# Turning the normalised rows on DVE, ACT and Pool instead of TensorE

## The chip, the cores and the metric

One core of one Trainium2 chip runs the whole program. The metric is the device time of one execution in microseconds, lower is better. All data are 32-bit floats.

## The reference

Attention with softmax over the feature axis of q and over the token axis of k, then a Fourier mix over tokens and channels, a normalisation without weights, and a two-layer channel network:

```python
batch, n_heads, seq, head_dim = (8, 8, 576, 64)        # so d_model = 512
q_s = softmax(q, axis=-1);  k_s = softmax(k, axis=2)   # each with 1e-09 added to the sum
kv = np.einsum('bhsd,bhde->bhse', ...)                 # k_s^T v, 64 x 64 per head
attn = np.einsum('bhsd,bhde->bhse', q_s, kv)
x = attn.transpose(0, 2, 1, 3).reshape(8, 576, 512)
mixed = np.real(np.fft.fft(np.fft.fft(x, axis=1), axis=2))
u = x + mixed
un = (u - u.mean(-1)) / np.sqrt(u.var(-1) + 1e-06)
out = u + np.maximum(un @ w_ch1, 0.0) @ w_ch2          # 512 -> 2048 -> 512
```

## The kernel before

**Groups.** The 8 x 576 rows are cut into nine groups of 512. Groups 0 to 7 (`g`) are 512 rows of one batch each, and group 8 collects the 64 rows that each of the eight batches leaves over. They run in the order 0 to 6, 8, 7; "order" counts the places, from 0. A group lies in SBUF as four tiles of 128 rows x 512 columns, tile `i` = (c, u) with c = i % 2 and u = i // 2, pairs of them in the `x` buffers (`xs` for group 8).

**Two stages per group.** `up` multiplies the normalised rows by the first weight matrix and applies relu; `down` multiplies by the second and adds to u. Both use Strassen's scheme with seven products, run in the order 1, 6, 5, 7, 2, 4, 3. Group 0 is plain. For the others `up` has eight jobs of seven products with right-hand blocks from `unT`, the normalised rows transposed: [128, 7, 2, 256], slots 0 to 3 the four quarters, slots 4, 1, 5 and 6 their differences (`combine`, `combine_last`). From order 2 on, `down` (`deep_down`) uses a second level of Strassen: product 1 alone, and then the units (2,4), (7,6) and (5,3), each of seven products for two members. Its left-hand sums ("A sums", `a_step`, L1407) are made by DVE (and one kind by Pool), and those of the unit (2,4) are written into the old `unT`, which `up` has left by then. So a new `unT`, of which there is one buffer, can be written only when PE has finished that unit.

**Banks.** Products of a unit gather in three PSUM banks: `ba` for 1 and 2, `bb` for 6, 7 and 4, `bc` for 5 and 3. What takes them out: after 1 ACT copies `ba` to `s1` (L1475); after 6 DVE forms u2 = bb + s1, after 7 u3 = bb + s1 and out(3) = bc + u3 (all L1468); after 2 ACT copies `ba` out, out(0) (L1482); after 4 and 3 DVE forms out(2) and out(1). Since product 7 adds into `bb` after 6, and 4 after 7, PE may start 7 only when u2 has been read, and 4 only when u3 has.

**Between the stages.** While PE runs `up` and `down` of one group, the other engines prepare the next one: attention (`keys`, `own_exp`, `own_times_kv`) during `up`, the folds and the Fourier mix (`folded`, `block`, `mix_own`, `mix_shared`) around the start of `down`, and `norm` late in `down`. `norm` takes the mean and variance of the four tiles on DVE (L1165, L1166), one root on ACT for all four (L1169, with a table load), 1/std and -mean/std on DVE (L1172, L1173), the normalised tile on ACT into a buffer `eo` (L1189), four 128x128 transposes of it on PE into PSUM (L1195), one copy on ACT into `unT` (L1204), and then the differences (L1210, L1215).

**Order.** The whole program is one list of (time, step), sorted by time, and each engine executes its own steps strictly in that order:

```python
    steps += [(before + scale * t, step) for t, step in later]
    ...
        for _, step in sorted(steps, key=lambda s: s[0]):
            step()
```

The times are only a script: they set the order of the steps on each engine, and semaphores do the rest. In `deep_down` one unit of script time (a "slot") stands for half a product, so `down` has slots 0 to 8 for product 1, 8 to 22 for (2,4), 22 to 36 for (7,6) and 36 to 50 for (5,3), and the next group's `up` begins at slot 50. Before the change `block` runs from slot 2, the mixes from 12.5, `norm` from 29. For order 1 `down` is a single level of Strassen with eight slots per product, 56 in all; for order 7, the last normalisation, `norm` starts at slot 14 before and after.

**A pattern already there.** `own_exp` turns q in 32x32 tiles on DVE (L764), and carries them to their quadrants of 32 partitions with 16 ACT instructions of 32x128 that also take the exponent (L774). The keys are turned on DVE too (L708).

**Keys and values.** `keys` multiplies the turned keys by values in `vt` (L715): r = 0 and 1 with the first half of the columns, r = 2 and 3 with the second half, which `values_to` loads into the same tile by four DMAs after r = 1.

Of the kernel before, what the change touches and what calls it, by code (L numbers as in the profile page):

```python
# [40 lines left out]
F32 = mybir.dt.float32  # L41
# [5 lines left out]
P = 128  # L47
B, H, S, DH = 8, 8, 576, 64
D = H * DH
# [3 lines left out]
HD = D // 2  # L53
# [5 lines left out]
Q = 32  # L59
W = 2 * Q  # L60
NT = Q // 2 + 1
KT = D // P
VD = 4 * NC - S // Q
NF = FF // P
GT = 4 * P
# [16 lines left out]
UP, TWICE = NP * len(ORDER), 8 + 6 * len(ORDER)  # L82
# [36 lines left out]
def at(t, script):  # L119
    return [(t + dt, step) for dt, step in script]  # L120
# [17 lines left out]
class _Block:  # L138
    def __init__(self, ctx, tc, q, kT, v, w1, w2, ft, cd, out):
# [24 lines left out]

        self.ZT = c.tile([P, KT, P], F32, name="ZT")

# [57 lines left out]
    def turned(self):  # L224
        t = self.ps.tile([P, 4, P], F32, tag="tr", name="tr", bufs=2)
        return t
# [102 lines left out]
    def weights(self):  # L329
# [6 lines left out]
        def fetch(i):  # L336
# [10 lines left out]
            if i < NF:  # L347
                nc.sync.dma_start(raw.rearrange("p (k n) -> p k n", k=KT), w1[:, :, f * 2 * P:(f + 1) * 2 * P])
            else:
# [129 lines left out]
    def attention_timed(self, b, start, end):  # L479

        tail = [("t", b)] if b % 2 == 0 else []
        own = [("q", b, c, u) for c, u in ((0, 0), (0, 1), (1, 1), (1, 0))]
        places, shared = [6, 13.5, 21.5, 27.2], start + 12
        if tail:
            places = [8.5, 14, 21.5, 27.2]
        if start == 0:
            places, shared = [13.5, 20.5, 24, 27.2], 7
        steps = at(start, self.keys(b))
        for it in tail:
            steps += at(shared, self.q_exp(it)) + at(shared + 8, self.t_turn(it))  # L490
            steps += at(22.4 if start < 0 else 35, self.t_fold(it))
        for t, it in zip(places, own):
            steps += at(t, self.own_exp(it)) + at(t + 15, self.own_times_kv(it))
        loads = [(t - 7, t + 7.6, self.own_load(it)) for t, it in zip(places, own)]
        loads += [(shared - 13, shared + 8.4, self.t_load(it)) for it in tail]
        loads.sort(key=lambda s: s[0])
        free = [-99] * 3
        for i, (t, end, load) in enumerate(loads):
            if i > 1:
                steps += at(max(t, free[-3]), load)  # L500
            free.append(end)
        return steps + at((33 if start < 0 else 39) if tail else max(22, start + 26), self.t_times_kv(b))

    def ahead(self, b):


        steps = at(24 if b > 2 else 20, self.keys_to(b))
        steps += at(35 if b > 2 else 22.5, self.values_to(b, 0))
        q = [self.own_load(("q", b, 0, u)) for u in range(2)]
        if b % 2 == 0:  # L510
            q = [self.t_load(("t", b)), q[0]]
        return steps + at(46.5, q[0]) + at(50, q[1])
# [129 lines left out]
    def values_to(self, b, h):  # L642

        def load(i):
            first = VD * (i == 3)
            a = min(i * NC, S // Q - NC) + first
# [5 lines left out]
    def prepare(self):  # L652
# [6 lines left out]
        for col in (0, 2 * P + 1):  # L659
            G.memset(self.vt[:, :, col:col + 1], 1.0)  # L660
        G.memset(self.vt[3 * Q:, 0:VD, :], 0.0)

# [20 lines left out]

        return [(0, copies), (0.3 + 0.15 * (4 // by), least)]

    def keys(self, b):


        nc, V, kb = self.nc, self.nc.vector, self.kb
        box = {}  # L690

        def top(r):
            if r == 0:
                box["m"] = self.small.tile([P, 4 * NR], F32, tag="km16", name="km16", bufs=2)
            V.reduce_max(box["m"][:, 4 * r:4 * r + 4], kb[:, r], axis=AX.X, negate=True)

        def exp(g):
            k = kb[:, g // 4, g % 4]
            nc.scalar.activation(k, k, ACT.Exp, bias=box["m"][:, g:g + 1])

        def turn(r):
            if r == 0:
                t = self.work.tile([P, KT, HD], F32, tag="Z", name="Z", bufs=1)
                t = t[:].rearrange("p k n -> p (k n)")[:, 0:NC * P]
            else:
                t = kb[:, r - 1].rearrange("p g s -> p (g s)")
            to = box["k", r] = t.rearrange("p (c n) -> p c n", n=P)
            V.transpose(to.rearrange("p c (g s) -> p c g s", s=Q), kb[:, r].rearrange("p g (c s) -> p c g s", s=Q))  # L708

        def times(r):  # L710
            pk, k = self.acc((P, P + 1)), box.pop(("k", r))
            box[r] = pk
            a = (P + 1) * (r % 2)
            for c in range(NC):
                nc.tensor.matmul(pk, lhsT=k[:, c, :], rhs=self.vt[:, c, a:a + P + 1], start=c == 0, stop=c == NC - 1)  # L715

        def scale(r):
            pk = box.pop(r)
            rec = self.small.tile([P, 1], F32, tag="krec", name="krec", bufs=4)
            at = P * (r % 2)  # L720
            V.tensor_scalar(out=rec[:], in0=pk[:, at:at + 1], scalar1=ATT_EPS, scalar2=None, op0=ALU.add)
            V.reciprocal(rec[:], rec[:])
            for h in range(2):
                s, cols = slice(64 * h, 64 * h + 64), slice(64 * h + 1 - r % 2, 64 * h + 65 - r % 2)
                V.tensor_scalar(out=self.kvr[b % 2][s, r, s], in0=pk[s, cols], scalar1=rec[s, 0:1], scalar2=None, op0=ALU.mult)

        steps = [(0.9 * r, lambda r=r: top(r)) for r in range(NR)]
        steps += at(3.6, self.across(lambda: box["m"], 2, 4 * NR)) + at(4.5, self.across(lambda: box["m"], 1, 4 * NR))
        steps += [(6 + g / 2, lambda g=g: exp(g)) for g in range(4 * NR)]
        for r in range(NR):  # L730
            for dt, f in ((8.3, turn), (10.8, times), (12.5, scale)):
                steps.append((dt + 2 * r + 6 * (r > 1 and f != turn), lambda f=f, r=r: f(r)))
        steps += at(13.5, self.values_to(b, 1))
        return steps

    def own_load(self, it):
# [330 lines left out]
    def block(self, b, k):  # L1067
# [6 lines left out]
        n = own.stop - own.start  # L1074
        if k == KT:

            own, tail = slice(own.start, own.start + P), slice(tail.start, tail.start + P)

        def times():
            eo, g = self.eo[b], self.live["g", b]  # L1080
            if b not in self.Z:
                self.Z[b] = self.work.tile([P, KT, HD], F32, tag="Z", name="Z", bufs=1)
            full = self.acc((own.stop - own.start, 512))
# [72 lines left out]
    def norm(self, g):  # L1156

        nc, V = self.nc, self.nc.vector
        mv = self.small.tile([P, 4, 2], F32, tag="mv", name="mv", bufs=2)
        std = self.small.tile([P, 4], F32, tag="std", name="std", bufs=2)  # L1160
        uns, box = {}, {}
# [36 lines left out]
        def laid(i):  # L1198
# [4 lines left out]
            copy = V.tensor_copy if g == 0 and c == u else nc.scalar.copy  # L1203
            copy(self.unT[g][:, u:u + 3:2, :, cols], box.pop(i)[:].rearrange("p (a k) t -> p a k t", a=2))  # L1204

        def combine():
            if g > 0:
                some = lambda i: self.unT[g][:, i]
                for e, to, x, y in ((V, 4, 1, 0), (nc.gpsimd, 1, 3, 1), (V, 5, 3, 4)):
                    e.tensor_tensor(out=some(to), in0=some(x), in1=some(y), op=ALU.subtract)  # L1210
# [5 lines left out]

        steps = []
        put = lambda t, f, *a: steps.append((t, lambda: f(*a)))
        if g == 0:
            for some in ((0, 2), (1, 3)):  # L1220
                s = slice(some[0], 4, 2)
                for i in some:
                    put(0, stats, i)
                for f in (root, scales):
                    put(0, f, s)
        else:
            for n, i in enumerate((0, 2, 1, 3)):
                put((0.7, 2.7, 4.7, 6)[n], stats, i)
            s = slice(0, 4)
            put(7.2, root, s)  # L1230
            put(9, scales, s)
            put(13.6, back)
# [391 lines left out]
def kernel(ctx: ExitStack, tc: tile.TileContext, q, kT, v, w1, w2, ft,  # L1624
                                                           cd, out):
    blk = _Block(ctx, tc, q, kT, v, w1, w2, ft, cd, out)

    def timed(t, order, g):
        b = order + 1
        steps = at(t, blk.up(order, g)) + at(t + UP, blk.down(g, order))  # L1630
        if order == B:
            return steps + [(t + 6 + 1.2 * i, lambda i=i: blk.later and blk.later.pop(0)()) for i in range(36)]
        if b == B:
            return steps + at(t + UP + 14, blk.norm(groups[b]))
        start, end = -7 if order > 2 else 0, 45
        if b + 1 < B:
            steps += at(t, blk.ahead(b + 1))
        steps += at(t, blk.attention_timed(b, start, end)) + at(t + end, blk.folded(b))
        t += UP
        for i, k in enumerate((2, 3, 0, 1, 4)):  # L1640
            steps += at(t + 2 + 2 * i, blk.block(b, k))
        mixes = [blk.mix_own(b, c) for c in range(2)]
        if b % 2:
            mixes.insert(0 if b == B - 1 else 2, blk.mix_shared(b // 2))
        for i, some in enumerate(mixes):
            steps += at(t + 12.5 + 3.2 * i, some)
        return steps + at(t + 29, blk.norm(groups[b]))

    fetch, convert = blk.weights()

# [26 lines left out]
    groups = [*range(B - 1), B, B - 1]  # L1677
    first, second, both = 46.9, 56, 77
    steps = blk.opening(fetch, converted)
# [3 lines left out]
    t = first + second  # L1683
# [26 lines left out]
    scale, before = 0.87, t + both  # L1710
    later = []
    t = 0
# [62 lines left out]
```

## Time and profile before

| | us |
|---|---|
| median of 3 runs (range) | 1054.22 (1052.79 to 1058.33) |
| the profiled execution | 1057.53 |
| its span, first to last instruction | 1055.8 |
| PE busy | 1037.7 (98%) |
| PE weight loads busy | 899.8 (85%) |
| DVE busy | 722.6 (68%) |
| ACT busy | 456.1 (43%) |
| Pool busy | 406.0 (38%) |

Matmuls are pipelined, so their durations overlap, and the time that one takes from PE's queue is the step from its start to the next start. A group of both stages takes about 112 us (`down` of order 3 starts at 473.35, that of order 4 at 584.21). Idle time in a row stands with what ended it. "PEld" is PE's weight load; a small q behind an engine is its sequencer.

### The profile page before, as it was taken

The numbers are of one execution on the slowest core, as the hardware profiler recorded it, in microseconds if no ns is written. First come the engines' busy times: TensorE is split into PE (matmuls) and PEld (weight loads), VectorE is DVE, ScalarE is ACT, GpSimd is POOL, SyncE is SP. The second block draws the span as 40 slices with busy tenths as digits, with TensorE's granted clock in tenths as the row PEclk, the third lists the DMA queues.
The fourth block names the chain that finished last, engine by engine and source line by source line (L and its number), as shares of the span: only waits on it lengthen the run. The fifth ranks groups of instructions, "written<-read, shape, count | busy, mean of one in ns | idle before, by whom it ended". The sixth has DMA issues, their size and how long they took to land.

```text
span 1055.8 us, 16768 instructions
## 1 busy us (share of the span) xinstructions
PE 1037.7 (98%) x6178; PEld 899.8 (85%) x6178; DVE 722.6 (68%) x1410; ACT 456.1 (43%) x1141; POOL 406.0 (38%) x350
## 2 busy tenths in 40 slices
PE   8999999899999999999999999999999999999998
PEld 7844555788888899889998999989998998999898
DVE  6898888665566876767765777688657644674563
ACT  5674433672248316751476236821682132131210
POOL 3164320257415645465545643474446450000000
PEclk9999999999999999999999999999999999999999
DMA  9787598586998666855677467757644664576464
GB/s 269 240 281 258 164 257 273 167 251 197 300 308 242 206 217 243 230 190 210 251 236 220 179 239 238 206 201 260 212 170 162 229 243 165 206 259 221 173 222 147
DMA packets 114313, 236.01 MB, mean 224 GB/s; under 512 B 23272, under 2 KB 78696, under 8 KB 103608
## 3 DMA queue, kind: packets, MB, share of 16 engines
q1 hardware_dynamic: 113864, 234.42, 67.7%
q8 instruction: 49, 0.80, 0.3%
q14 instruction: 32, 0.26, 0.1%
q10 hardware_dynamic: 288, 0.26, 0.1%
q0 software_dynamic: 80, 0.26, 0.1%
HBM read 199.79 MB, written 39.06 MB: 226 GB/s over the span
## 4 chain that ended last, share of the span: by engine, by line
PE 78%; DVE 5%; ACT 4%; DMA 3%; issue 1%; SPq 0%; POOL 0%; DVEq 0%; ACTq 0%
PE bb L1334 14%; PE bb L1461 10%; PE ba L1334 10%; PE bc L1334 9%; PE bc L1461 7%; PE ba L1461 7%; PE bb L1431 5%; PE acc L715 3%; ACT qT L774 2%; PE bb L1550 2%; PE acc L790 2%; PE acc L1087 1%; PE acc L1090 1%; DMA vt<-in_v_dram 1%; PE bc L1550 1%; PE ba L1550 1%
## 5 line engine op out<-in xcount | busy, mean ns | idle before, releaser
L1334 PE MATMUL bb<-unT,big 128*128 128x256 f32 x768 | 183.1, 381 | 0.1
L1334 PEld LDWEIGHTS bb<-unT,big 128*128 128x128 f32 x768 | 144.7, 191 | 19.9 <-DVE u L1304 1.0
L1346 ACT ACTIVATE big<-big 128x512 f32<-128x512 f32 x96 | 60.3, 629 | 170.8 <-DVE big L1345 169.9
L1334 PE MATMUL ba<-unT,big 128*128 128x256 f32 x512 | 124.0, 379 | 0.2 <-ACT big L1341 0.2
L774 ACT ACTIVATE qT<-q 32x128 f32<-32x128 f32 x384 | 117.9, 307 | 12.1 <-DVE q L764 7.1
L1334 PE MATMUL bc<-unT,big 128*128 128x256 f32 x512 | 121.8, 380 | 0.5 <-DVE big L1345 0.5
L1304 DVE TENSOR_TENSOR u<-bb,s 128x512 f32<-128x512 f32 x66 | 45.4, 687 | 94.5 <-PE bb L1334 79.5
L1334 PEld LDWEIGHTS bc<-unT,big 128*128 128x128 f32 x512 | 96.1, 190 | 14.2 <-DVE big L1345 1.8
L1334 PEld LDWEIGHTS ba<-unT,big 128*128 128x128 f32 x512 | 94.8, 190 | 12.6 <-ACT big L1341 0.6
L1461 PE MATMUL bb<-big 128*128 128x128 f32 x848 | 105.1, 275 | 0.3 <-DVE u L1468 0.3
L1461 PEld LDWEIGHTS bb<-big 128*128 128x128 f32 x848 | 99.6, 192 | 0.5 <-DVE u L1468 0.4
L1411 POOL TENSOR_TENSOR x<-x,big 128x512 f32<-128x512 f32 x45 | 57.7, 1296 | 63.5 <-DVE big L1468 31.2
L1461 PE MATMUL ba<-big 128*128 128x128 f32 x640 | 79.6, 275 | 0.0
L1461 PEld LDWEIGHTS ba<-big 128*128 128x128 f32 x640 | 76.3, 192 | 1.2
L1407 DVE TENSOR_TENSOR big<-big 128x512 f32<-128x512 f32 x98 | 75.3, 806 | 0.0
L761 POOL TENSOR_TENSOR q<-q,qm 128x512 f32<-128x512 f32 x24 | 25.8, 1073 | 116.1 <-DVE qm L756 73.0
L1210 POOL TENSOR_TENSOR unT<-unT 128x512 f32<-128x512 f32 x8 | 14.1, 1769 | 124.6 <-DVE unT L1210 124.6
L1468 DVE TENSOR_TENSOR u<-bb,s 128x256 f32<-128x256 f32 x40 | 16.8, 420 | 64.8 <-PE bb L1461 61.5
L1431 PE MATMUL bb<-big 128*128 128x256 f32 x256 | 58.7, 381 | 0.0
L384 POOL TENSOR_TENSOR big<-big 128x512 f32<-128x512 f32 x24 | 30.4, 1268 | 71.0 <-ACT big L1346 71.0
L1345 DVE TENSOR_TENSOR big<-bc,u 128x512 f32<-128x512 f32 x64 | 44.0, 687 | 18.6 <-PE bc L1334 17.8
L1431 PEld LDWEIGHTS bb<-big 128*128 128x128 f32 x256 | 48.2, 190 | 8.0 <-DVE big L1345 1.1
(279 smaller groups left out, 2032.2 us busy)
## 6 DMA issues: line engine op xcount, KB each, us to landing
big<-w2d SPq DMA_DIRECT2D x67, 1024.0 KB
big<-w1s SPq DMA_DIRECT2D x64, 896.0 KB
big<-w2s SPq DMA_DIRECT2D x16, 1024.0 KB
big<-in_w_dram SPq DMA_DIRECT2D x21, 512.0 KB
w2d<-big SPq DMA_DIRECT2D x42, 256.0 KB
kb<-in_kT_dram SPq DMA_DIRECT2D x24, 320.0 KB
q<-in_q_dram SPq DMA_DIRECT2D x28, 256.0 KB
vt<-in_v_dram SPq DMA_DIRECT2D x36, 160.0 KB
```

The lines of the kernel that those rows point to most:

```text
L384: e1.tensor_tensor(out=to(4), in0=at(2), in1=at(3), op=ALU.add)
L715: nc.tensor.matmul(pk, lhsT=k[:, c, :], rhs=self.vt[:, c, a:a + P + 1], start=c == 0, stop=c == NC - 1)
L774: nc.scalar.activation(to[t, i * Q:i * Q + Q], one, ACT.Exp)
L1304: plus = lambda t: V.tensor_tensor(out=temp(t), in0=box["bb"][:], in1=box["s1"][:], op=ALU.add)
L1334: nc.tensor.matmul(bank()[:, i, :], lhsT=w[:, WA_AT[m], k * P:(k + 1) * P], rhs=self.unT[g][:, B_AT[m], k, :], start=first and i == 0 and ...
L1345: steps = [(0, lambda: V.tensor_tensor(out=hp(i), in0=bank()[:], in1=u()[:], op=ALU.add)), (0.8, lambda: nc.scalar.activation(hp(i), hp(i) ...
L1346: (0.8, lambda: nc.scalar.activation(hp(i), hp(i), ACT.Relu))]
L1407: e.tensor_tensor(out=to(o), in0=to(x), in1=to(y), op=op)
L1411: E.tensor_tensor(out=x, in0=x, in1=tile(m), op=ALU.add)
L1431: nc.tensor.matmul(box[name][:, i, :], lhsT=h[p][:, A_AT[m], i * P:(i + 1) * P], rhs=self.stream[n][:, p, :], start=p == 0 and (m != 1 or ...
L1461: nc.tensor.matmul(box[place[n]][:, i, :], lhsT=own(m)(A_AT[n])[:, f, :], rhs=w[:, r // 2, r % 2 * P:r % 2 * P + P], start=first and f == ...
L1550: nc.tensor.matmul(bank()[:, i, :], lhsT=h[p][:, A_AT[m], i * P:(i + 1) * P], rhs=w[:, p, :], start=first and i == 0 and p == 0, stop=p == ...
```

## The change

For groups 2 to 8 `norm` no longer transposes on PE. The normalised tile is turned in place by one DVE instruction in 32x32 blocks (`turned`), and 16 copies of 32x128 bring the blocks to their quadrants in `unT` (`moved`): 13 on ACT and 3 on Pool (`ON_POOL`). The statistics, root and scales are taken in two pairs of tiles instead of four at once. `norm` begins at slot 17.2 instead of 29 (20.5 for order 1), its last `combine` steps come some four slots earlier, the mixes begin at 9.2 instead of 12.5, and the blocks at 0, 1.7 apart, instead of 2, 2 apart (both as before for order 1). In `keys` the products, scales and second value loads are moved back by 1.5 slots, and for order 1 the products r = 2 and 3 by two more; key loads of groups 3 and 4 are issued 3 slots later. Groups 0 and 1 keep their transposes on PE.

```diff
+ON_POOL = (3, 8, 13)
...
-        steps = at(start, self.keys(b))
+        steps = at(start, self.keys(b, start))
...
-        return steps + at((33 if start < 0 else 39) if tail else max(22, start + 26), self.t_times_kv(b))
+        return steps + at((33 if start < 0 else 39) if tail else max(22, start + 29), self.t_times_kv(b))
...
-        steps = at(24 if b > 2 else 20, self.keys_to(b))
+        steps = at(20 if b == 2 else 27 if b < 5 else 24, self.keys_to(b))
...
-            for dt, f in ((8.3, turn), (10.8, times), (12.5, scale)):
-                steps.append((dt + 2 * r + 6 * (r > 1 and f != turn), lambda f=f, r=r: f(r)))
-        steps += at(13.5, self.values_to(b, 1))
+            for dt, f in ((8.3, turn), (12.3, times), (14, scale)):
+                steps.append((dt + 2 * r + (6 + 2 * (start == 0)) * (r > 1 and f != turn), lambda f=f, r=r: f(r)))
+        steps += at(15, self.values_to(b, 1))
...
+        def turned(i):
+            V.transpose(uns[i][:, 0:D], uns[i][:, 0:D])
+
+        def moved(i, some):
+            if g not in self.unT:
+                self.unT[g] = self.work.tile([P, 7, 2, HD], F32, tag="unT", name="unT", bufs=1)
+            c, u = i % 2, i // 2
+            of = uns[i][:, 0:D].rearrange("p (a k t s) -> t p a k s", a=2, k=2, t=4)
+            for n in some:
+                j, t = n // 4, n % 4
+                copy = nc.gpsimd.tensor_copy if n in ON_POOL else nc.scalar.copy
+                copy(self.unT[g][t * Q:t * Q + Q, u:u + 3:2, :, c * P + j * Q:c * P + j * Q + Q], of[t, j * Q:j * Q + Q])
...
+        if g > 1:
+            for n, (i, k) in enumerate(((0, 2), (1, 3))):
+                t = 6.5 * n
+                put(t, stats, i)
+                put(t + 1, stats, k)
+                put(t + 2, root, slice(i, 4, 2))
+                put(t + 3.2, scales, slice(i, 4, 2))
+            each = 4.8
+            for n, i in enumerate((0, 2, 1, 3)):
+                t = 4.2 + each * n
+                put(t, normal, i)
+                put(t + 1.3, turned, i)
+                for k in range(8):
+                    put(t + 2 + 0.5 * k, moved, i, (2 * k, 2 * k + 1))
+            put(5 + 4 * each, back)
+            put(3.5 + 4 * each + 2, combine)
+            put(13.5 + 4 * each + 2, combine_last)
+            return steps
...
-        t += UP
+        t, soon = t + UP, 2 * (order == 1)
         for i, k in enumerate((2, 3, 0, 1, 4)):
-            steps += at(t + 2 + 2 * i, blk.block(b, k))
+            steps += at(t + soon + (1.7 if order > 1 else 2) * i, blk.block(b, k))
...
-            steps += at(t + 12.5 + 3.2 * i, some)
-        return steps + at(t + 29, blk.norm(groups[b]))
+            steps += at(t + 9.2 + 1.65 * soon + 3.2 * i, some)
+        return steps + at(t + 17.2 + 1.65 * soon, blk.norm(groups[b]))
```

More of the change, by code (lines that the diff above doesn't have):

```diff
@@ L684, in across, with keys @@
         return [(0, copies), (0.3 + 0.15 * (4 // by), least)]
-    def keys(self, b):
+    def keys(self, b, start):
         nc, V, kb = self.nc, self.nc.vector, self.kb
```

## The prediction

> **What bounds the kernel now.** I read the page, then PE's timeline in a middle group, the groups by line, the timelines of ACT and DVE, and PE's waits.
>
> ```profile
> span 1055.8 us, 16768 instructions
> ...
> PE 1037.7 (98%) x6178; PEld 899.8 (85%) x6178; DVE 722.6 (68%) x1410; ACT 456.1 (43%) x1141; POOL 406.0 (38%) x350
> ```
>
> TensorE is the bound. PE's timeline (start, duration, count at the end) in the second stage that runs from 473.35 to 526.72:
>
> ```profile
> 510.68 1.95 PE L1461 MATMUL bc<-big 128*128 128x128 f32 x16
> 512.47 1.95 PE L1461 MATMUL ba<-big 128*128 128x128 f32 x16
> ...
> 516.94 0.60 PE L1195 MATMUL tr<-ident,eo 128*128 128x128 f32 x4
> 517.37 1.06 PE L1461 MATMUL bc<-big 128*128 128x128 f32 x8
> ```
>
> Read starts, for matmuls overlap: a product of 16 takes 1.787 us of the queue, so one slot of the script (half a product) is 0.894 us; four transposes take 516.94 to 517.37, 0.109 us each. No gap stands between them: work taken out here is gained, and a wait put in here is lost.
>
> The nearest relatives of what is added, in the groups by line (busy, mean ns, idle before):
>
> ```profile
> L774 ACT ACTIVATE qT<-q 32x128 f32<-32x128 f32 x384 | 117.9, 307 | 12.1 <-DVE q L764 7.1
> L764 DVE STREAM_TRANSPOSE q<-q 128x512 f32<-128x512 f32 x24 | 17.0, 707 | 3.2 <-POOL q L761 2.9
> ```
>
> And two rows of ACT's timeline, for the step from one instruction to the next:
>
> ```profile
> 210.91 2.56 ACT L774 ACTIVATE qT<-q 32x128 f32<-32x128 f32 x8
> 530.01 3.61 ACT L699 ACTIVATE kb<-kb,km 128x160 f32<-128x160 f32 x11
> ```
>
> Eight L774 fill 2.56 us: a step of 0.32, nothing overlapped. Eleven L699 of 0.416 each fill 3.61: a step of 0.32 too, so these overlap by 0.095.
>
> **What goes, per group.** 16 transposes leave PE: 16 x 0.109 = 1.75 us on the path. Four evictions (L1204, 0.58 each, 2.3 us) leave ACT, which is busy 15.8 of the stage's 53.4 us: nothing by itself.
>
> **What comes.** Four DVE turns of 0.71 us, 52 copies on ACT, 12 on Pool, a second root. ACT copies cost as L774 (also 32 partitions to another quadrant, 128 elements): 0.318 a step. Whether they fit is a question of one chain, counted from zero at the boundary of slot 22, where the unit (2,4) ends. The A sums of that unit lie in the old unT, so no copy can start earlier.
>
> *When the first copy starts.* DVE's queue decides. It is in order, and its timeline of before gives the steps:
>
> ```profile
> 493.69 0.42 DVE L1468 TENSOR_TENSOR u<-bb,s 128x256 f32<-128x256 f32 x1 [3.00 <-PE bb L1461]
> 494.15 0.42 DVE L1468 TENSOR_TENSOR big<-bc,u 128x256 f32<-128x256 f32 x1
> 494.49 0.75 DVE L1132 TENSOR_TENSOR eo<-acc,sn 128x256 f32<-128x256 f32 x2
> 495.15 0.15 DVE L1133 COPY eo<-acc 128x2 f32<-128x2 f32 x1
> 495.22 1.28 DVE L1407 TENSOR_TENSOR big<-big 128x512 f32<-128x512 f32 x2
> 496.42 0.42 DVE L1144 TENSOR_TENSOR x<-x,eo 128x257 f32<-128x257 f32 x1
> ```
>
> The change's order puts behind u3 (it waits for slot 16, so it starts at -5.36 + 0.2 = -5.16): u3 and out(3) 0.79, sums 0.73, two A sums (L1407) 1.20, two statistics (L1165 and L1166) 1.62, two adds (L1144 and L1145) 1.32, out(2) 0.34, reciprocal and scale 0.46. That is 6.46, to 1.30; then ACT's normalisation 0.81, the turn 0.71, hand-overs 0.2: the first copy starts at 3.0. Bounds: 1.3 (only out(1) and the turn behind slot 22) and 5 (L1407 and L1173 also show 1.75 and 1.16 us where Pool works beside them). I take 3.0, as Pool is mostly idle there.
>
> *How long ACT needs.* 52 x 0.318 = 16.5; three more normalisations 2.4; two s1 copies and one out(0) (L1475, L1482, 0.37) 1.1; root 0.3: 20.3, to 23.3. The turns of tiles 2 to 4 hide behind the three copies left of the tile before. Pool's twelve: bounds 0.2 us (as L678's 32x16 on ACT) and 0.66 (L952, 128x256 with two inputs); with 0.66 Pool ends its last at about 22, under ACT's cover, and without that cover it would be the one that ends last. Behind a waiting copy stand s1 on ACT (needed by u2, up to 3 us late) and `into` and the A sums of the unit (5,3) on Pool, which slot 49 needs first.
>
> *Who waits.* On DVE the first difference of `combine` waits for the last copy, and behind it in the queue stand the second (0.60 each), a key maximum (L695, 0.75) and u3 of the unit (5,3), 0.42: 2.4 us, to 25.7. u3 must have read bank bb before PE's product 4 may write it at slot 46: 24 x 0.894 = 21.45. **PE waits 4.3 us per group**; lesser waits for u2 and u3 on the way are part of that total, for it is one lateness.
>
> *Sum.* Groups of order 2 to 5: 4.3 - 1.75 = 2.5 each. Moving the blocks up adds 0.2: the third now comes 5.4 us after the stage starts (a single's 1.73, two blocks of 0.98, 1.73 again), and DVE's L1055, which it needs, ended 5.6 after it. 4 x 2.7 = 11. Order 6 has one more mix between u3 and the turn, some 0.95 more: 3.7. Order 7 (the last normalisation) has no mixes, its copies start at 0.2 and end at 20.5, but `combine` stands ahead of u2: 20.5 + 1.2 + 0.6 + 0.5 = 22.8 against slot 42 (17.9), 4.9 - 1.75 = 3.1. Order 1 works in 128x256 products, PE stays 6.9 us on each, `combine` has no bank behind it that is needed before the next first stage: the whole 1.75 is gained.
>
> *Keys and values.* The first row is of PE's list of waits (us, times, longest), the second of the windows (busy time by engine, then PE's granted clock, the DMAs' share and GB/s):
>
> ```profile
> PE acc L715 <- DMA vt<-in_v_dram: 2.8, 2, 2.7
> ```
>
> ```profile
> 203.60:207.10 3.50, 3.50 (x14) 3.23 (x15) 0.00 (x0) 0.00 (x0) 0.33 (x1) 0.51 0.27 111
> ```
>
> PE waited 2.65 us, and then its granted clock was 0.51 for 3.5 us, worth 1.7 more. The change moves the waiting product 3.5 slots (3.0 us) later, the values' four DMAs 1.5 slots (1.3 us, as the product that frees the tile moves too): the wait falls to about 1 and the slow clock goes with it, -3. The DMAs stand on SP behind weight loads that wait for their own buffers, so the bounds are 0 and -4.4. Key loads for two groups go 3 slots back, 70 slots ahead of their use: nothing, and 1 us of DMA if that cover were gone.
>
> All: 11 + 3.7 + 3.1 - 1.75 - 3 = +13. The profiled execution took 1057.53 us (span 1055.8 and 1.7 around it) and would take 1070.5; it stands 3.3 above the median of 1054.22, so the median forecast is **1067**.
>
> **A rule against the row.** The step of 0.318 carries all this. The Trainium skill, "ScalarE: Activation LUTs", section "What ACT_TABLE_LOAD costs", gives 186 ns + 0.833 ns an element for an ACTIVATE without pointer operands, and has back-to-back ones overlap by about 93 ns. By it a copy would step at some 200 ns (an estimate from that page), and the sum would be the first rival's. The trace agrees on L699 (0.095) and disagrees on L774.
>
> **Rivals.**
> 1. *The copies overlap.* As L699 does: 0.307 - 0.095 = 0.212 a step, 11.0 us instead of 16.5. Then 3.0 + 14.8 + 2.4 = 20.2, before slot 46: no wait. 112 transposes x 0.109 = 12.2 gained, and 3 at the values: 1054 - 15 = 1039. For it: no row is quite this copy, and a quarter of the copies stay in their quadrant. Against: the two 32-partition rows, L774 and L678 (four of 0.201 in 0.84), both change quadrants and neither overlaps. The point that decides: with the other terms as they are (9.2 us), a step under 0.236 leaves no wait, and one of 0.27 eats just what the transposes give.
> 2. *The first copy starts early,* at 1.3, as DVE runs ahead of its rows. The wait is 2.6, a group costs 1.05, orders 2 to 6 5.3, the rest -1.65: +3.6, 1058, no change. Against: every term ahead of the turn is in program order.
> 3. *The wait halves PE's clock too.* The 2.65 us wait did, the 1.5 us one at 163.5 did not. Most of the 4.3 falls at slot 46 in one piece; 1.7 more in six groups: 1077. The Trainium skill, "TensorE: Matmul & The Clock Gate", Part 1, has a block set the clock by how busy PE was of late; the trace agrees with 0.51 after the wait.
>
> **How the numbers follow.** A measurement here can tell about 0.5% (5.3 us) from no change. The forecast has 0.52, rival 3 0.13, rival 1 0.23, rival 2 0.12. So slower 0.65, same 0.12, faster 0.23. The forecast's own range, by first copies from 2 to 4 us and steps from 0.306 (L678's 0.201 and 112 more elements at 0.83 ns) to 0.33, is 1058 to 1078, rival 3 within it. For 8 in 10 the range must reach into rival 1: 1040 to 1078.
>
> **What would show it.** Right: 32 transposes of L1195 instead of 144; ACT copies (L1218) of about 0.3 us without overlap; DVE's `unT` L1224 waiting for ACT's L1218; PE idle 2 to 4 us at `bb` in the last unit of six groups, for DVE's u3. Wrong: copies that step at 0.2, or L1224 done before slot 43, and PE without a gap; then the time is near 1040. A wait for `vt` still over 2.5 us, or for Pool's copies, would each break one term.

## The result, and the profile after

The changed kernel takes 1072.46 us (median of 4, 1071.74 to 1072.86), the kernel before 1054.43 in the same comparison: ratio 1.0167, 95% interval 1.0145 to 1.019. It is slower, by 1.5 to 1.9%. The profiled execution took 1072.86 us, its span is 15.3 us longer than the one before.

The head of the page, and the copies in its groups by line:

```profile
span 1071.1 us, 17062 instructions
...
PE 1035.2 (97%) x6066; PEld 895.4 (84%) x6066; DVE 729.9 (68%) x1452; ACT 554.0 (52%) x1484; POOL 431.6 (40%) x434
```

```profile
L1218 ACT COPY unT<-eo 32x128 f32<-32x128 f32 x364 | 107.6, 295 | 13.3 <-DVE eo L1208 6.1
L1218 POOL COPY unT<-eo 32x128 f32<-32x128 f32 x84 | 30.4, 361 | 146.5 <-DVE eo L1208 79.9
```

PE has 112 instructions less, as planned, and lost more by waiting. The row for that in PE's list of waits (total, times, longest), before and after; the row for `vt` that stood in the list of before is gone:

```profile
PE bb L1461 <- DVE u L1468: 0.3, 1, 0.3
```

```profile
PE bb L1493 <- DVE u L1500: 22.7, 22, 3.2
```

Three timelines of `down` of order 3 show the chain that the prediction counted. The boundary of slot 22 is at 494.70 here. ACT, first and last copies:

```profile
498.59 0.61 ACT L1218 COPY unT<-eo 32x128 f32<-32x128 f32 x2 [0.85 <-DVE eo L1208]
...
514.52 3.98 ACT L1218 COPY unT<-eo 32x128 f32<-32x128 f32 x13
```

DVE, where L1224 is the first two differences of `combine`, L696 a key maximum, and L1500 u3 of the unit (5,3):

```profile
518.61 1.42 DVE L1224 TENSOR_TENSOR unT<-unT 128x512 f32<-128x512 f32 x2 [3.65 <-ACT unT L1218]
519.94 0.81 DVE L696 TENSOR_REDUCE km<-kb 128x4 f32<-128x640 f32 x1
520.67 0.41 DVE L1500 TENSOR_TENSOR u<-bb,s 128x256 f32<-128x256 f32 x1
```

PE's waits in that stage, at slots 28, 32, 42 and 46:

```profile
501.03 2.05 PE L1493 MATMUL bb<-big 128*128 128x128 f32 x16 [0.52 <-DVE u L1500]
...
505.63 2.05 PE L1493 MATMUL bb<-big 128*128 128x128 f32 x16 [0.76 <-DVE u L1500]
...
515.01 2.05 PE L1493 MATMUL bb<-big 128*128 128x128 f32 x16 [0.18 <-DVE u L1500]
...
521.14 3.47 PE L1493 MATMUL bb<-big 128*128 128x128 f32 x16 [2.29 <-DVE u L1500]
```

Read upwards from the last row: PE may write bank bb when u3 is read (520.67 and 0.41), u3 stands behind the differences and the key maximum, the differences wait 3.65 us for ACT, and ACT has been at work without a pause since the first copy. From start to start, where a matmul's own drain counts too, the four waits cost 0.68, 0.92, 0.34 and 2.45 us: 4.4 for the group.

The last row's duration, 3.47 instead of 2.05, is a second loss: half clock. The profile shows it in stretches of 3.41 us, which start at 405.47, 521.52, 753.63 and 965.25 here, whole multiples of 3.413 us apart. On the grid that these starts give, the window that holds the wait of order 3 and the next window, then the two windows into which the same wait falls one group on (columns: window, length, busy time by engine with PE first, PE's granted clock, the DMAs' share, GB/s):

```profile
518.11:521.52 3.41, 1.12 (x10) 0.93 (x9) 2.85 (x6) 2.13 (x5) 2.15 (x2) 1.00 0.65 250
521.52:524.93 3.41, 3.41 (x18) 3.41 (x18) 2.67 (x6) 0.90 (x5) 2.08 (x2) 0.50 0.11 24
634.16:637.57 3.41, 1.62 (x15) 1.43 (x13) 2.00 (x3) 2.97 (x8) 1.74 (x2) 1.00 0.77 269
637.57:640.98 3.41, 2.91 (x26) 2.92 (x27) 3.04 (x6) 0.29 (x2) 2.96 (x3) 1.00 0.18 29
```

Half clock followed in the groups of orders 2, 3, 5 and 7, some 1.63 us each; not in orders 4 and 6. The wait of order 4 is as long as that of order 3, 2.29 us, but it lies across a boundary of the grid: PE stood idle for 1.79 us of one window and for 0.50 of the next. The traces of all twelve kernels here agree on where the limit lies. Behind their first 15 us, each of the 18 windows at full clock in which PE stood idle for 2.04 us or more was followed by half clock, and none with 1.93 or less. (Idle is what the profile's ends of matmuls leave.)

The whole account, from start to start of PE's instructions: the span without PE's gaps fell from 1031.8 to 1019.9 us (112 transposes at 0.109 are 12.2); lost time, which is what a step takes over the usual one of its shape, rose from 24.0 to 51.2, of which the waits of six groups are 26.5, half clock 6.5 and the third block of five groups 1.4, and the stretch from 150 to 250 us, with `vt`, lost 6.8 less.

### The profile page after: what moved, and what is told of

Read it like the earlier page. It is cut to its first block, busy times and chain, and to the rows that moved or that the text cites. A ratio compares the mean times of both kernels' runs of the same rounds, so it can differ in the third digit from the quotient of the medians.

```text
span 1071.1 us, 17062 instructions
## 1 busy us (share of the span) xinstructions
PE 1035.2 (97%) x6066; PEld 895.4 (84%) x6066; DVE 729.9 (68%) x1452; ACT 554.0 (52%) x1484; POOL 431.6 (40%) x434
## 4 chain that ended last, share of the span: by engine, by line
PE 70%; DVE 12%; ACT 12%; DMA 4%; issue 2%; SPq 1%; POOL 0%; DVEq 0%; ACTq 0%; POOLq 0%
PE bb L1366 15%; PE ba L1366 10%; PE bc L1366 10%; ACT unT L1218 8%; PE bb L1463 5%; PE bb L1493 4%; PE bc L1493 2%; PE acc L716 2%; PE ba L1493 2%; PE bb L1582 2%; PE acc L791 2%; ACT eo L1190 2%; PE bb L1282 2%; PE ba L1282 2%; PE bc L1282 2%; DVE x L1146 2%
## 5 line engine op out<-in xcount | busy, mean ns | idle before, releaser
L1493 PE MATMUL bb<-big 128*128 128x128 f32 x848 | 110.4, 285 | 22.8 <-DVE u L1500 22.7
L1493 PEld LDWEIGHTS bb<-big 128*128 128x128 f32 x848 | 102.6, 198 | 27.7 <-DVE u L1500 27.2
L1218 ACT COPY unT<-eo 32x128 f32<-32x128 f32 x364 | 107.6, 295 | 13.3 <-DVE eo L1208 6.1
L1218 POOL COPY unT<-eo 32x128 f32<-32x128 f32 x84 | 30.4, 361 | 146.5 <-DVE eo L1208 79.9
L1443 POOL TENSOR_TENSOR x<-x,big 128x512 f32<-128x512 f32 x45 | 60.3, 1349 | 35.0 <-ACT big L1470 18.8
L1439 DVE TENSOR_TENSOR big<-big 128x512 f32<-128x512 f32 x98 | 66.0, 697 | 0.0
L1463 PEld LDWEIGHTS bb<-big 128*128 128x128 f32 x256 | 48.2, 190 | 8.3 <-DVE big L1377 1.1
```

Source lines behind the costliest of these rows:

```text
L1218: copy(self.unT[g][t * Q:t * Q + Q, u:u + 3:2, :, c * P + j * Q:c * P + j * Q + Q], of[t, j * Q:j * Q + Q])
L1439: e.tensor_tensor(out=to(o), in0=to(x), in1=to(y), op=op)
L1443: E.tensor_tensor(out=x, in0=x, in1=tile(m), op=ALU.add)
L1463: nc.tensor.matmul(box[name][:, i, :], lhsT=h[p][:, A_AT[m], i * P:(i + 1) * P], rhs=self.stream[n][:, p, :], start=p == 0 and (m != 1 or ...
L1493: nc.tensor.matmul(box[place[n]][:, i, :], lhsT=own(m)(A_AT[n])[:, f, :], rhs=w[:, r // 2, r % 2 * P:r % 2 * P + P], start=first and f == ...
```

## The experiments

The first four ran together (before: 1056.08 there), then three (1055.37), then one at a time.

### Where the differences stand: e1

```diff
-            put(3.5 + 4 * each + 2, combine)
+            put((30.1 if g == B - 1 else 26.9), combine)
```

> The changed kernel with one step later in the order: the first differences of unT (combine) stand behind u3 and out(3) of the last unit, at slot 44.1, instead of 41.9 (for the last normalisation 44.1 instead of 38.7). Theory A (PE waits because DVE sits in combine for ACT's last copy, with u3 queued behind it): the 2.45 us wait at slot 46 goes in orders 2 to 5, 1.7 in order 6, about 2.5 in order 7, and with it the slow clock that followed in four groups (1.6 each); the waits at slots 28, 32 and 42 (0.7, 0.9, 0.3) stay, as they have other causes. About 1072.5 - 20.5 = 1052. Rival B (the copies are too late for the next first stage itself, and combine only shows it): PE waits as long at slot 50 or 52, for unT, and the time stays near 1070. Rival C (PE is slowed by something else than this wait, such as the slow clock by itself): between.

Measured: 1053.5 us, ratio 0.9985 (0.997 to 1.0001). DVE's rows of order 3 show the new order: u3 first, then the differences.

```profile
516.45 0.42 DVE L1500 TENSOR_TENSOR u<-bb,s 128x256 f32<-128x256 f32 x1 [1.42 <-PE bb L1493]
...
517.98 1.70 DVE L1224 TENSOR_TENSOR unT<-unT 128x512 f32<-128x512 f32 x2
```

The wait at slot 46 and every half clock are gone with one step's place in a queue, 19 us in all by the medians. The copies are not quicker; nobody on PE's path waits for them any more. Part of the gain is lost again to a wait of 2.2 us for first-stage weights at 342 us, which is new. The three smaller waits stay as they were, so they have another cause:

```profile
PE bb L1493 <- DVE u L1500: 8.7, 16, 1.3
```

### The places without the turn: e2

The changed kernel with `norm`'s old branch (16 transposes on PE) in the new places:

```diff
-        if g > 1:
+        if g > B:
```

> The changed kernel with the transposes of groups 2 to 8 back on PE, and nothing of the turn on DVE: blocks, mixes, norm and keys stay at their new places. Theory A: without the copies ACT and DVE have slack again, so no wait at the last unit; the transposes cost their 12.2 us; the wait for vt and its slow clock (4.5 us together) stay away; the third block of five groups still waits 0.3. About 1054.4 - 4.5 + 1.8 = 1052. Rival (moving mix and norm up is itself what crowds DVE and delays u2 and u3): PE waits at bb for DVE in the units (7,6) or (5,3), 1058 or more.

Measured: 1054.54, ratio 0.999 (0.998 to 1.0001). Against e4 below, which has the same keys and values and the old places, moving the blocks, mixes and norm up costs 5.3 us by itself. One u late by 0.5 or 0.9 us in each of five groups and 0.28 at the third block in four of them make up 4.3 of it. The time lies between theory and rival, nearer to the theory: the wait is the one that the rival named, at a smaller price. It also means that e1's turn on DVE is worth no more than 1 us against e2, which the two intervals do not tell from nothing, although it takes 12.2 us of transposes off PE: the turns and their order bring the rest back as waits.

### The step of a copy: e3 and e7

In e3 each copy writes the quadrant that it reads, so that the blocks lie in wrong places; number and size of the copies are the same.

```diff
-                copy(self.unT[g][t * Q:t * Q + Q, u:u + 3:2, :, c * P + j * Q:c * P + j * Q + Q], of[t, j * Q:j * Q + Q])
+                copy(self.unT[g][j * Q:j * Q + Q, u:u + 3:2, :, c * P + t * Q:c * P + t * Q + Q], of[t, j * Q:j * Q + Q])
```

> The changed kernel with each copy writing the quadrant it reads (block j,t goes to rows j and columns t, so the blocks lie in the wrong places of unT); the number, size and order of the copies are the same. Theory A, with the cause of the step in the change of quadrant from one copy to the next: 9 of 13 copies per tile follow one of the same quadrants and overlap by 0.1, a mean step of about 0.23 instead of 0.306, ACT ends its copies 3.9 us earlier, one of the 4.4 us of waits per group is left, no slow clock: about 1045. Rival (a 32-partition copy never overlaps the one before, whatever its quadrants): step 0.306, time 1072.

Measured: 1051.66, ratio 0.9959 (0.9946 to 0.9972). Thirteen copies, which took 3.98 us in the changed kernel:

```profile
498.38 3.06 ACT L1218 COPY unT<-eo 32x128 f32<-32x128 f32 x13
```

The step is about 0.20 us between copies of one quadrant, and stays about 0.306 at each change: 0.23 in the mean. The waits at slots 42 and 46 and the half clocks go, as ACT ends early. But the time is 7 us above what was expected of it: the one at slot 28 stays at 0.7, and the one at slot 32 grows from 0.92 to 1.36.

e7 puts the same copies, blocks in their right places, in the order of the quadrant that is written:

```diff
-                j, t = n // 4, n % 4
+                t, j = n // 4, n % 4
```

> The changed kernel with the same copies in another order: the four copies of a tile that follow each other write one quadrant and read four, where they read one and write four. Where e3 kept both quadrants the step was 0.20 us. If the quadrant written decides whether two copies overlap: 3 of 4 steps are 0.20 us, ACT's 52 copies take 13 us instead of 16, the wait at slot 46 goes and the time is 1051 to 1055. If the quadrant read decides or both must stay: 0.31 us a step as now, and 1072.

Measured: 1071.84, ratio 1.0148 (1.0128 to 1.0167), and 13 copies take as long as in the changed kernel:

```profile
502.15 3.98 ACT L1218 COPY unT<-eo 32x128 f32<-32x128 f32 x13
```

So neither the quadrant read nor the one written is enough: two copies overlapped only where both stayed, which a carry across quadrants never has between neighbours of one tile.

### Another engine for the copies: e6

```diff
-ON_POOL = (3, 8, 13)
+ON_POOL = (1, 3, 6, 8, 11, 13)
```

> The changed kernel with 24 instead of 12 of a group's 64 copies on Pool. Theory (ACT's row of copies sets when the differences start): ACT has 12 x 0.306 = 3.7 us less, its last copy is at about 20.1 us after slot 22 instead of 23.8, the differences are past by 22.5 us, and the wait at slot 46 (21.4 us) falls from 2.5 us to about 1, the one at slot 42 stays; the half clocks go: 1054 to 1060. Rival (Pool takes ACT's place as the last: 24 copies of 0.36 us and its `into` steps of 1.2 us between them end later than ACT): the wait at slot 46 stays or grows and the time is 1070 to 1080.

Measured: 1077.13, ratio 1.0201 (1.0183 to 1.022), as the rival said. DVE's first difference now waits for Pool, whose copies stand between its `into` steps of 1.27 us, and the wait at slot 46 is longer than with ACT:

```profile
520.30 2.36 DVE L1224 TENSOR_TENSOR unT<-unT 128x512 f32<-128x512 f32 x2 [5.54 <-POOL unT L1218]
```

```profile
523.77 3.78 PE L1493 MATMUL bb<-big 128*128 128x128 f32 x16 [4.17 <-DVE u L1500]
```

### The keys and values alone: e4

The kernel before, with only the changes in `keys`, in the start of `t_times_kv` and in the key loads' slots.

> The kernel before with only the keys' part of the change: products, scales and second value loads 1.5 slots later, 2 more for r = 2 and 3 in order 1, key loads of two groups 3 slots later. If that part alone takes the 2.65 us wait for vt and the 3.4 us of slow clock behind it away: 1054.4 - 4.5 = 1050. If the wait goes away only because the blocks, mixes or transposes moved: 1054.

Measured: 1049.23, ratio 0.9939 (0.9922 to 0.9956): faster than both kernels. The wait for `vt` and the slow clock behind it are gone, 6.9 us of median against this batch's before. What it brings is a wait of 1.5 us for first-stage weights at 342 us (L1334, for the DMA of `big<-w1s`), which is not in the list of before.

### An order in which the turn pays: e5, e8, e9, e10

If every wait is a u2 or u3 behind other work of DVE, there should be an order of the same work without them. All four keep e1's idea for the differences, start order 7's norm 3 slots later and spread the blocks over 0, 1.7, 4.1, 6.1 and 6.8. They differ in `norm`, whose new order holds for all of groups 2 to 8. The first:

```diff
+            put(8.4, stats, 1)
+            put(9.3, stats, 3)
...
+            for i, t in ((0, 4.2), (2, 4.25), (1, 13.8), (3, 13.85)):
                 put(t, normal, i)
+            for i, t in ((0, 5.5), (2, 8.35), (1, 18.4), (3, 18.45)):
+                put(t, turned, i)
```

> The changed kernel with the norm of groups 3 to 8 put in another order: each normal and each turn starts only when DVE has done the u2 and u3 of its slot, the blocks of `second` lie further apart, the differences stand behind the u3 of slot 44, and the norm of the last order starts 3 slots later. Theory (every wait of the changed kernel is one of DVE's u behind something else): the waits at slots 28, 32, 42 and 46 fall from about 4.4 us to under 1 us per group, order 7 loses under 2 us, no half clock follows, and the transposes stay away: 1049.2 (keys alone) - 12.2 (transposes) + 0 to 7 = 1037 to 1044. Rival (DVE has no room, and the waits only move to other slots or to the loads of w1): 1049 to 1056.

Measured: 1071.56, ratio 1.0155 (1.0135 to 1.0175): a miss beyond the rival's range. DVE's rows of order 3 (line numbers are two higher in this and the next three) show why. The first u2 is that of slot 28, the last row the u3 of slot 32:

```profile
498.19 0.42 DVE L1502 TENSOR_TENSOR u<-bb,s 128x256 f32<-128x256 f32 x1 [0.57 <-ACT s L1509]
498.53 0.70 DVE L1208 STREAM_TRANSPOSE eo<-eo 128x512 f32<-128x512 f32 x1
499.16 0.65 DVE L1166 BATCH_NORM_STATS2 st<-x 128x6 f32<-128x512 f32 x1
...
499.94 1.54 DVE L1441 TENSOR_TENSOR big<-big 128x512 f32<-128x512 f32 x1
501.41 0.68 DVE L1166 BATCH_NORM_STATS2 st<-x 128x6 f32<-128x512 f32 x1
...
502.22 3.21 DVE L1441 TENSOR_TENSOR big<-big 128x512 f32<-128x512 f32 x3
505.36 0.41 DVE L1502 TENSOR_TENSOR u<-bb,s 128x256 f32<-128x256 f32 x1
```

The two u stand 7.2 us apart in DVE's queue and four slots, 3.6 us, apart on PE. The four A sums (L1441) alone are 4.75 here, and these had been overlooked when the statistics were put between them. One alone takes 0.68, so some 2 of the 4.75 us are a slowing: Pool is in sums of its own (499.67 to 502.62, 503.24 to 506.56) for most of that time. PE lost 3.34 us at slot 32, and half clock followed.

e8 takes all statistics ahead of the first turn, leaves one turn behind the u2 of slot 28 and puts three behind the u3 of slot 32; the copies of two tiles alternate.

```diff
+            for t, i in ((0, 0), (1, 2), (4.5, 1), (4.9, 3)):
+                put(t, stats, i)
...
+            for i, t in ((0, 8.35), (2, 12.35), (1, 13.3), (3, 13.8)):
+                put(t, turned, i)
```

> The changed kernel with the norm of groups 3 to 8 in a second new order, after the trace of e5, where two row statistics and a turn stood between the u2 of slot 28 and the u3 of slot 32: now all four statistics are ahead of the first turn, one turn stands behind the u2 of slot 28, the other three behind the u3 of slot 32, the differences behind the u3 of slot 44; the copies of two tiles alternate, so that every second copy keeps the quadrants of the one before. Theory (each wait is a u2 or u3 behind DVE work of the change): no wait over 0.5 us at slots 28 to 46, no half clock, 1049.2 - 12.2 + 0 to 7 = 1037 to 1044; the step from a copy to the next one with the same quadrants is 0.20 us, the others 0.31. Rival (DVE is full between slots 24 and 36 whatever the order, so that what is moved out of one wait comes back in the next): 1049 to 1060.

Measured: 1048.24, ratio 0.9926 (0.9897 to 0.9955): 4 us above the expected range, just under the rival's 1049. Two losses were left in most groups, 0.9 to 1.2 us at slot 32 and 1.06 in the next `up`. The second is not ahead of its first product, as the next expectation has it, but ahead of its fourth, product 7, which waits for u2 (525.04 in order 3). Where copies of two tiles alternate, every second one keeps both quadrants, and the steps are 0.20 and 0.30 by turns. In the middle of this row one tile's copies are alone and step at 0.31, so that its mean is 0.277:

```profile
504.62 5.00 ACT L1218 COPY unT<-eo 32x128 f32<-32x128 f32 x18
```

e9 puts the first turn ahead of the u2 of slot 28, and the statistics, root and scales of the second half late:

```diff
+            for t, i in ((0, 0), (1, 2), (4.5, 1), (12.35, 3)):
+                put(t, stats, i)
...
+            for i, t in ((0, 4.2), (2, 4.25), (1, 14), (3, 14.05)):
                 put(t, normal, i)
+            for i, t in ((0, 4.8), (2, 8.35), (1, 16.35), (3, 18.35)):
+                put(t, turned, i)
```

> The kernel of e8 with the first turn ahead of the u2 of slot 28 and the statistics and scales of the second half behind the u3 of slot 32, so that only one turn (0.7 us) and four sums of `a_step` stand between that u2 and that u3, and ACT's copies start some 1.5 us earlier. e8 lost 0.87 to 1.19 us per group at slot 32 and 1.06 us ahead of the first product of the next group. Theory (the first is DVE's 1.0 us of turn and scales, the second the keys that stand behind the differences on DVE, and these wait for ACT's last copy): the first falls to about 0.5 and the second goes: 1048.2 - 5 x (0.4 + 1.06) = 1040 to 1043. Rival (the keys' sums are late for their own place, not for the differences; and the sums beside Pool take 1.6 us instead of 0.7 wherever the turn is): 1046 to 1049.

Measured: 1054.4, ratio 0.9993 (0.9978 to 1.0008). Both losses shrank, to 0.27 us at slot 32 in orders 3 and 5 (0.92 in 2 and 4, 0.50 in 6) and to nothing in the next `up`, and a new one came that the theory had not foreseen, with half clock behind it in order 4. ACT's rows of order 3, then PE's:

```profile
505.25 1.52 ACT L1190 ACTIVATE eo<-x,mv,std 128x512 f32<-128x512 f32 x2 [0.97 <-DVE mv L1174]
506.68 0.35 ACT L1516 COPY big<-ba 128x256 f32<-128x256 f32 x1
```

```profile
507.08 2.05 PE L1495 MATMUL ba<-big 128*128 128x128 f32 x16 [2.05 <-ACT big L1516]
```

Two normalisations wait for DVE's scales, and out(0), which PE needs at slot 36, stands behind them: 2.2 us in five groups, and 1.0 in the last order. e10 moves these two alone:

```diff
-            for i, t in ((0, 4.2), (2, 4.25), (1, 14), (3, 14.05)):
+            for i, t in ((0, 4.2), (2, 4.25), (1, 14.9), (3, 14.95)):
```

> The kernel of e9 with one step moved: the normals of the second half stand behind the copy of out(0) on ACT, not ahead of it. In e9 the wait at slot 32 fell to 0.3 us and the one ahead of the next group went, but six times PE waited 2.1 to 2.2 us at slot 36 for out(0), which stood behind two normals that waited for their scales. Theory (that wait is of the order on ACT alone): it goes, and no other comes: 1054.4 - 11 = 1042 to 1045. Rival (the normals, now late, pass the wait on to s1 or to the u2 of slot 42): 1046 to 1052.

Measured: **1044.85**, ratio 0.9905 (0.9889 to 0.9922), the fastest here: 10.5 us under before, and about 4 under e4, whose interval it touches, so that what the turn itself brings is only just clear of the noise. From its page:

```profile
PE 1023.2 (98%) x6066; PEld 887.9 (85%) x6066; DVE 746.3 (72%) x1452; ACT 543.7 (52%) x1484; POOL 440.2 (42%) x434
```

The span without PE's gaps is 1019.8 us, as in the changed kernel; the lost time is 22.4 us instead of 51.2, nearly half of it in the first 150 us. The wait of 0.9 us at product 7 of the next `up`, absent in e9, is back in four groups, against the theory's "no other comes".

## Why the prediction was right, and where its terms were off

The forecast was 1067, the time is 1072.46, inside the forecast's own range. Of the 5.5 us between them, some 2.3 lie in the terms below, which compare the profiled executions. The rest is the step from there to the median: the execution of before stood 3.3 us above its median and the forecast kept that distance, but the one of after stands only 0.4 above its own. The mechanism is the one forecast, on the path named: first copy, ACT's row, differences, u3, bank bb, slot 46. e1 shows the last link by moving it, e3 and e6 the one before it by shortening ACT's row or handing the end to Pool.

| term, us over the kernel | predicted | measured |
|---|---|---|
| transposes off PE | -12.2 | -11.9 (all of PE's work) |
| waits, orders 2 to 5 | 4 x 4.3 = 17.2 | 4 x 4.4 = 17.7 |
| waits, order 6 | 5.3 | 3.3 |
| waits, order 7 | 4.9 | 5.6 |
| third block | 1.0 | 1.4 |
| keys and values | -3 | -6.8 |
| half clock after the waits | not in the forecast | 6.5 |
| sum | +13 | +15.3 (with -0.5 in small differences) |

That the sum came so near is partly luck: 6.5 us of half clock were left out, and 3.8 at the keys and 2.0 in order 6 were off the other way.

*First copy.* Predicted 3.0 us after slot 22, measured 3.9. The step that failed is the start of the row, "it waits for slot 16, so it starts at -5.36 + 0.2 = -5.16": u3 began at 490.56, which is -4.14, for DVE came late to it. The adds of the mixes ahead of it took 1.49 us instead of 0.42, twice a group in orders 2 to 5, and each time Pool was in a sum of its own and the add ended 0.3 us behind that sum. "Pool is mostly idle there" holds from u3 to the first copy (Pool has no row from 490.36 to 498.64), and not ahead of it. DVE, then Pool:

```profile
486.80 1.49 DVE L1146 TENSOR_TENSOR x<-x,eo 128x255 f32<-128x255 f32 x1
...
489.15 1.48 DVE L1146 TENSOR_TENSOR x<-x,eo 128x255 f32<-128x255 f32 x1
```

```profile
486.62 1.38 POOL L1439 TENSOR_TENSOR big<-big 128x512 f32<-128x512 f32 x1 [3.10 <-DVE big L1439]
489.04 1.32 POOL L1439 TENSOR_TENSOR big<-big 128x512 f32<-128x512 f32 x1 [1.03 <-DVE big L1439]
```

*ACT's row.* Predicted 20.3 us, measured 19.9 (498.59 to 518.50): the step is 0.306, not 0.318, which is the range's lower end. The last copy was to end 23.3 us after slot 22 and ended at 23.8.

*The wait.* It is one lateness, as forecast. ACT had no pause between the first copy and the last, so what PE lost on the way moved nothing behind it. PE came to slot 46 26.4 us after slot 22 instead of 21.45, 5.0 late where the forecast had 4.3; the four waits are 4.4 of it, and the rest lies in single steps, 0.19 at slot 24 and 0.1 behind each wait. The errors of the first copy (+0.9), of ACT's row (-0.4) and of the tail behind it (+0.2) partly cancel. What the prediction did not see is that the waits on the way have a cause of their own: e1 left 0.7, 0.92 and 0.34 us of them standing when slot 46 had none, so that moving the differences could win back only 2.45 of the 4.4. They belong to DVE: the turns, statistics and A sums ahead of u2 and u3, as e5, e8 and e9 showed by moving them.

*Order 6.* The third mix did hold the turn back, by 0.7 us (its tile was ready at 845.40, the turn began at 846.14). But Pool was not beside the adds ahead of it, DVE was not late, and the first copy came 3.2 us after slot 22, earlier than in order 3; the last ended at 23.1. The forecast's tail also had a key maximum of 0.75 between the differences and u3, and in this order none stands there. *Order 7* lost most at slot 42 as forecast (3.4), and 2.2 more at two u's before it.

*Half clock.* This is the rival with 0.13, and it was mostly right: four of six groups paid 1.63 us. Left out of the forecast, it accounts for 6.5 of the 15.3. Length alone does not decide, for waits of 2.29 us went both ways. In these traces it is the idle time within one window of the grid, with a limit between 1.93 and 2.04 us; the 2.65 us wait that the prediction cites lay in one window, and so did the one of 1.5, which is under the limit. The grid lies elsewhere in each execution, and e7, with the same waits, was hit in three groups (from 520.69, 752.80 and 964.42). The Trainium skill, "TensorE: Matmul & The Clock Gate", Part 1, ties the clock to how busy PE was of late; the rows agree, as half clock only ever follows a gap.

*Keys and values.* The wait of 2.65 was to fall to about 1; it went altogether, with the slow clock behind it and smaller ones near by. e4 shows it apart, at 1049.23 against the 1056.08 before of its batch, 6.9 by medians; -3 was too careful.

*Against the rivals.* The copies do not overlap, as the rows L774 and L678 said; e3 and e7 show that this hangs on the quadrants and not on the operation. The rule that the prediction weighed (the Trainium skill, "ScalarE: Activation LUTs", section "What ACT_TABLE_LOAD costs", about 93 ns of overlap back to back) holds where both quadrants stay: 0.306 less 0.20 is some 0.1. In its own price that rival was too hopeful: with a mean step of 0.23 e3 lost the wait at slot 46, as the prediction's point of 0.236 has it, but came to 1051.66, not 1039, for the waits at slots 28 and 32 are not ACT's. The early first copy did not happen.

## What to carry to other kernels

Work taken off the bounding engine is gained only if the engine that takes it over has room in the very slots where the bound waits for it: count the queue between two of its deadlines (here 3.6 us between two u's on DVE), not its mean load of 68%. Before copying faster or elsewhere, look at what stands in the queue behind the instruction that waits for the copies, and move that; it was worth 19 us here for one line. A change of many parts should be taken apart: its side edits to the keys and values were worth 6.9 us, more than the part in its name gave even in its best order.

## What the runs showed of the hardware that was not expected

ACT's copies of 32x128 overlap by 0.1 us only if the neighbour reads and writes the same quadrants as the one before (steps of 0.20 and 0.306); alternating two tiles with the same pair of quadrants gets half of it (0.20 and 0.30 by turns, e8). A DVE sum with two inputs of 128x255 in SBUF took 1.07 us more beside a Pool sum that had just started, and ended 0.3 us after it, twice in each group of orders 2 to 5 of the changed kernel, and not in order 6. Half clock comes in stretches that start on a grid of 3.413 us: whether a wait of PE is followed by one depends on how much of it falls into one window of that grid. Behind the first 15 us of these twelve traces, 2.04 us or more in a window at full clock was followed by it every time, and 1.93 or less never. So the same wait of 2.29 us was followed by half clock in three groups and by full clock in a fourth, in the same place of the same program.
